# A table of rank offsets for a list-scheduled attention and two-MLP kernel

## The chip, the cores and the metric

The kernel runs on one core of a Trainium2 chip. The time is device microseconds of one launch; the time before is the median of three runs. A profile is one more execution of the same program, recorded by the hardware profiler, and its span is the time from the first to the last instruction.

## What is computed

Attention over 4 batches, 8 heads, 576 positions and 64 channels, in which each row of scores keeps only what lies within `tau` of its maximum, is followed by two multilayer perceptrons with 512 channels and 2048 hidden units, over 2304 tokens. Everything is in float32.

```python
def _attn_ref(q, k, v, tau):
    scores = np.matmul(q, k.transpose(0, 1, 3, 2)) / np.sqrt(q.shape[-1])
    thresh = np.max(scores, axis=-1, keepdims=True) - tau
    scores = np.where(scores >= thresh, scores, -1000000000.0)
    attn = np.exp(scores - np.max(scores, axis=-1, keepdims=True))
    attn = attn / (np.sum(attn, axis=-1, keepdims=True) + 1e-09)
    return np.matmul(attn, v)

def _moe_ref(x, w_in, w_out, s, b):
    r = np.maximum(x @ w_in, 0.0)
    return (s * (r * r) + b) @ w_out

def _moe2_ref(x, w_in, w_out, alpha):
    h = x @ w_in
    return (np.maximum(h, 0.0) + alpha * np.minimum(h, 0.0)) @ w_out
```

## The kernel before, in words

The kernel doesn't issue its work where the code names it. The code describes 7186 steps with `Plan.add` (L131): for each the engine that may run it, an estimate of its duration, the buffers it reads and writes, and a rank. A few kinds may go to one of two engines. `Plan.run` (L154) then goes through a made-up time: whenever an engine is free it takes, of the steps whose inputs are there, the one of the lowest rank, if buffers for it are free, and issues its instructions. Two steps of equal rank go in the order in which they were named. So the result is one fixed order of instructions per engine. On the chip each engine works through its own order, and a step whose input is late holds up all that stands behind it on that engine. The engines are TensorE (PE), VectorE (DVE), ScalarE (ACT), GpSimd (POOL) and SyncE (SP), which issues nearly all DMAs.

The ranks set what counts as urgent. In the attention there are 144 turns, one for each 128 query rows of a pair of heads. Each has a score matmul (L799), a maximum (DVE, L809), an exponential (ACT, L813), a threshold with sum (DVE, L815), transposes through TensorE (L317 and L319), split copies into a high and a low part (ACT and DVE, L952 to L985) and products with the values (L919). The turns are ten ranks apart, so an offset of 10 is one turn. The first four pairs of heads run in plain float32, the others in split float32r. The weights of the first perceptron are read as 64-bit words and converted (`numbers`, L406: a load, L408, then steps at L424 to L437). Their ranks run from 50 on, so that they come in beside the attention.

The perceptrons use three matmuls per product (`mm3`, L540 to L542: low by high, high by low, high by high). Blocks of the first perceptron have rank 1,000,000 and more, and fill TensorE when the attention has nothing for it. From about 500 us on the products of the remaining blocks stand in a chain, each named as coming after the one before (`full[0]`), so the order on TensorE is given there. They are Strassen products in Winograd's form: seven products of half the size, with sums of operands made on DVE and POOL (L505, L1249, L1254), split copies (L517, L518), and sums of results. The latter go so: a product lands in a bank, ACT copies it out (`copy`, L1440, rank `SOON` = -1, into one of at most six tiles of a group called q), and a later product adds onto the same bank, which it may do only after that copy. DVE adds the copy to another bank (`plus`, L1444, rank -1), and `leaky` (L1400) then makes the activation with two steps of ACT and one of DVE (L1405 to L1407, rank -1) and a store (L1409). Nearly everything off TensorE has rank -1 in this part, so the order of naming decides there.

Beside it run the loads of the activations of the next blocks (`load_x`, L546, DMA issue at L551, rank -1), whose halves are added by L1249. There are also the second perceptron's weights, converted to float32 and written back (`whole`, L524, ranks from 200, the multiplication at L424 on ACT or DVE), and the closing steps of the first perceptron's blocks (`outs_of`, L1171: a load of a partial result at L1184, a bias on ACT at L1186, a sum on DVE at L1188, a store at L1191).

A step's number is its place in the order of the calls of `Plan.add`, from 0. The numbers below were found by counting those calls; the order on each engine that results was laid beside the trace. The steps that are spoken of are these: 3920 and 3921, load and multiplication (L424) of one block of weights; 4455 to 4460, loads of activations (L551); 4855 and 4856, load (L1184) and bias step (L1186) of a partial result; 5221, 5340, 5413 and 5979, copies of a product (L1440); 5415 and 5416, the sum (L1444) and first activation step (L1405) of another; 5968, 5969, 5974 and 5975, activation steps; 5451, 5454, 5469 and 5472, split copies (L517); 3939 and 3945, multiplications like 3921 of later blocks of weights.

## Time and profile before

| | us |
|---|---|
| median of 3 runs | 1095.63 |
| lowest and highest | 1094.72, 1096.96 |
| the profiled execution, its own time | 1097.13 |
| its span | 1095.3 |
| TensorE, matmuls busy | 1068.3 (98%) |
| TensorE, weight loads busy | 1011.0 (92%) |
| VectorE busy | 913.7 (83%) |
| ScalarE busy | 785.6 (72%) |
| GpSimd busy | 360.6 (33%) |

The busy times are unions over the span. Matmuls overlap in the pipeline and their ends are modelled, so a matmul that is listed as busy may in part be waiting. The idle time of an engine is what is left of the span. A wait is put down to the instruction whose semaphore came last.

### The profile page before, as it was taken

The page shows a single profiled execution, that of the slowest core. Times are in us where ns is not written, and L with a number is a line of the kernel's source. Part 1 is how long each engine was busy: PE and PEld are TensorE (multiplying, and loading weights), DVE is VectorE, ACT ScalarE, POOL GpSimd, SP SyncE. Part 2 cuts the span into 40 slices and gives each one's busy share as a digit, 9 for nine tenths or more (in the row PEclk, how much of TensorE's full clock was granted, in tenths as well). Part 3 has the DMA queues.
Part 4 walks back from the last instruction along what each step waited for, and adds up shares of the span by engine and source line. Part 5 has one row for each costly group of instructions (what it writes and reads, how often), then busy time and mean ns, then how long its engine had stood idle before and what let it go on. Part 6 is the DMA issues. An engine that isn't in the chain of part 4 may idle for free.

```text
span 1095.3 us, 21723 instructions
## 1 busy us (share of the span) xinstructions
PE 1068.3 (98%) x7070; PEld 1011.0 (92%) x7070; DVE 913.7 (83%) x2075; ACT 785.6 (72%) x1873; POOL 360.6 (33%) x495
## 2 busy tenths in 40 slices
PE   9999999999999999999999999999999999999998
PEld 8777799999989888889999989999999999999998
DVE  4889888888888878848788898799899999998872
ACT  4898888887787778745656676777878997555551
POOL 1455654564575456520000122140102332112111
PEclk9999999999999999999999999999999999999999
DMA  5755375556546454325346976267776564564531
GB/s 119 197 174 161 90 180 136 126 139 187 132 109 162 118 132 99 98 92 183 110 149 225 286 257 201 81 210 251 249 246 224 162 210 137 156 165 126 149 88 39
DMA packets 197489, 174.06 MB, mean 159 GB/s; under 512 B 73472, under 2 KB 175872, under 8 KB 197376
## 3 DMA queue, kind: packets, MB, share of 16 engines
q1 hardware_dynamic: 195072, 171.05, 54.0%
q10 hardware_dynamic: 2304, 1.64, 0.6%
q8 instruction: 55, 0.90, 0.4%
q14 instruction: 58, 0.48, 0.1%
HBM read 100.54 MB, written 50.86 MB: 138 GB/s over the span
## 4 chain that ended last, share of the span: by engine, by line
PE 72%; DVE 10%; DMA 7%; ACT 6%; issue 3%; POOL 0%; SPq 0%; DVEq 0%; ACTq 0%; POOLq 0%
PE bank L540 11%; PE bank L541 11%; PE bank L542 11%; PE bank_b L540 7%; PE bank_b L541 6%; PE bank_b L542 6%; PE bank L919 6%; PE sc L799 6%; PE bank L319 3%; PE bank L317 3%; DMA stg<-in_moe_w_out_dram 2%; DVE e L815 1%; DMA stg<-in_moe_w_in_dram 1%; DVE mx L809 1%; ACT e L813 1%
## 5 line engine op out<-in xcount | busy, mean ns | idle before, releaser
L815 DVE SCALAR_TENSOR_TENSOR e<-sc,mx,e 128x576 f32<-128x576 f32 x144 | 116.1, 812 | 19.2 <-ACT e L813 14.5
L809 DVE TENSOR_REDUCE mx<-sc 128x1 f32<-128x576 f32 x144 | 106.7, 751 | 18.6 <-PE sc L799 17.8
L813 ACT ACTIVATE e<-sc,mx 128x576 f32<-128x576 f32 x144 | 106.1, 743 | 12.9 <-DVE mx L809 12.0
L540 PE MATMUL bank<-gt,wa 128*128 128x384 f32 (+4 forms) x256 | 89.2, 348 | 0.3 <-ACT rest L1065 0.3
L319 PE MATMUL bank<-eyes_r,e 128*128 128x128 f32 (+1 forms) x320 | 89.1, 286 | 0.3 <-DVE e L815 0.3
L540 PE MATMUL bank<-xt,wa 128*128 128x480 f32 (+3 forms) x223 | 84.0, 377 | 5.5 <-ACT gw L1440 4.0
L542 PE MATMUL bank<-gt,wa 128*128 128x384 f32 (+4 forms) x256 | 86.1, 336 | 0.0
L541 PE MATMUL bank<-gt,wa 128*128 128x384 f32 (+4 forms) x256 | 86.0, 336 | 0.0
L541 PE MATMUL bank<-xt,wa 128*128 128x480 f32 (+3 forms) x223 | 75.3, 338 | 0.0
L542 PE MATMUL bank<-xt,wa 128*128 128x480 f32 (+3 forms) x223 | 75.3, 337 | 0.0
L811 POOL TENSOR_SCALAR mx<-mx,tau_s 128x1 f32<-128x1 f32 x144 | 45.6, 317 | 83.1 <-DVE mx L809 77.4
L919 PE MATMUL bank<-gl,vt 128*128 128x256 f32 (+1 forms) x192 | 64.3, 336 | 1.0 <-DVE gl L977 0.7
L919 PE MATMUL bank<-gh,vt 128*128 128x256 f32 (+1 forms) x192 | 57.3, 300 | 1.2 <-ACT gh L975 0.4
L799 PE MATMUL sc<-k,q 128*128 128x288 f32 x264 | 54.7, 335 | 1.2 <-DVE e L815 0.8
L987 POOL TENSOR_TENSOR gr<-gf,gh 64x256 fp32r<-64x256 f32 (+1 forms) x48 | 39.2, 817 | 41.9 <-DVE gl L985 34.4
L540 PEld LDWEIGHTS bank<-xt,wa 128*128 128x128 f32 x223 | 43.1, 193 | 10.1 <-ACT gw L1440 3.0
L977 DVE TENSOR_TENSOR gl<-bank,gh 128x256 fp32r<-128x256 f32 (+1 forms) x96 | 43.4, 452 | 9.8 <-ACT gh L975 8.7
L540 PEld LDWEIGHTS bank<-gt,wa 128*128 128x128 f32 x256 | 49.1, 192 | 1.2 <-ACT rest L1065 0.5
L542 PEld LDWEIGHTS bank<-gt,wa 128*128 128x128 f32 x256 | 48.4, 189 | 1.7
L541 PEld LDWEIGHTS bank<-gt,wa 128*128 128x128 f32 x256 | 48.5, 190 | 0.8
L319 PEld LDWEIGHTS bank<-eyes_r,e 128*128 128x128 f32 (+1 forms) x320 | 44.5, 139 | 4.6 <-DVE e L815 0.7
L975 ACT ACTIVATE gh<-bank 128x256 fp32r<-128x256 f32 (+1 forms) x96 | 39.6, 412 | 11.4 <-PE bank L319 9.9
(729 smaller groups left out, 4203.5 us busy)
## 6 DMA issues: line engine op xcount, KB each, us to landing
stg<-in_moe_w_in_dram SPq DMA_DIRECT2D x32, 512.0 KB, 4.2
stg<-in_moe_w_out_dram SPq DMA_DIRECT2D x32, 512.0 KB, 4.1
gf<-gw SPq DMA_DIRECT2D x41, 192.0 KB, 2.5
q<-hq SPq DMA_DIRECT2D x24, 256.0 KB, 3.9
qo<-hq SPq DMA_DIRECT2D x24, 256.0 KB, 4.7
gw<-gf SPq DMA_DIRECT2D x48, 128.0 KB, 3.0
xt<-xs SPq DMA_DIRECT2D x13, 384.0 KB, 5.4
yat<-ya SPq DMA_DIRECT2D x24, 192.0 KB, 3.8
```

Source lines behind the costliest of these rows:

```text
L319: nc.tensor.transpose(to, part(x), one)
L540: nc.tensor.matmul(o, lhsT=wl, rhs=mh, start=first, stop=False, skip_group_check=on_top)
L541: nc.tensor.matmul(o, lhsT=wh, rhs=ml, start=False, stop=False, skip_group_check=on_top)
L542: nc.tensor.matmul(o, lhsT=wh, rhs=mh, start=False, stop=last, skip_group_check=on_top)
L799: nc.tensor.matmul(sp.t[:, x, :HS], lhsT=o[0][:, c], rhs=o[1][:, x * HS:(x + 1) * HS], start=n == 0, stop=n == len(passes) - 1)
L809: add("DVE", dve(S), lambda sp=sp, mx=mx: nc.vector.tensor_reduce(mx.t[:, 0:1], sp.t[:, :, :HS], op=ALU.max, axis=AX.XY, negate=True), (sp ...
L811: t2 = add("POOL", 0.26, lambda mx=mx: nc.gpsimd.tensor_scalar(mx.t[:, 1:2], mx.t[:, 0:1], -1.0, tau_s, op0=ALU.mult, op1=ALU.subtract), ( ...
L813: add("ACT", act(S, 1), lambda sp=sp, mx=mx, e=e: nc.scalar.activation(halves(e.t), sp.t[:, :, :HS], AF.Exp, bias=mx.t[:, 0:1]), (sp, mx), ...
L815: add("DVE", dve(S) + 0.065, lambda sp=sp, mx=mx, e=e, col=col, sums=sums: nc.vector.scalar_tensor_tensor(halves(e.t), sp.t[:, :, :HS], mx ...
L919: nc.tensor.matmul(o.t[:, :n], lhsT=w.rearrange("p a b -> p (a b)"), rhs=m.t[:, :n], start=c == first and x == 0, stop=c == last and x == ...
L975: add("ACT", act(n), lambda hi=hi, gt=gt: nc.scalar.activation(hi.t[:, :n], gt.t[:, :n], AF.Copy), (gt,), (hi,), rank=rank)
L977: add("DVE", dve(n), lambda hi=hi, lo=lo, gt=gt: nc.vector.tensor_tensor(lo.t[:, :n], gt.t[:, :n], f32(hi.t[:, :n]), op=ALU.subtract), (gt ...
```

## The change

A table `MOVES` is added that gives 2473 of the 7186 steps an offset in rank, 1230 of them positive (later) and 1243 negative (earlier), from 0.0001 to over 100 in size. `Plan.add` adds the offset to the rank of each way in which the step may run. Nothing else is changed: the same steps, instructions, buffers and transfers. Of the table only the lines stand here that hold the steps named in the text, and its first and last line.

```diff
--- before.py
+++ after.py
@@ -45,6 +45,228 @@
 FIRST_CS = (0, 2), (1, 3)
 SECOND_FS = (0, 1, 3, 2, 4, 5)
 LATER = 1e6
+MOVES = {
+    62: 2.91, 63: 2.63, 65: 19.4, 66: 19.4, 67: 15.5, 68: 15.5, 69: 12.3, 70: 12.3, 71: 14.1, 74: 2.32, 76: 0.114, 96: 0.472, 98: 0.822, 99: 1.41,
...
+    3892: -17.7, 3896: -1.88, 3897: 0.276, 3898: -3.45, 3899: -3.08, 3900: -1.48, 3901: -3.45, 3919: -15.3, 3920: 30.8, 3921: 1.38, 3922: -6.27,
...
+    4442: 0.626, 4443: -6.73, 4444: 0.0143, 4447: -6.13, 4448: 0.0143, 4452: 0.0143, 4453: -6.57, 4454: 17.2, 4455: 29.8, 4456: 30.9, 4457: 31.3,
...
+    4458: 13.9, 4459: 37.2, 4460: 28.6, 4461: -26.5, 4462: -51, 4463: 1.45, 4464: -31.4, 4471: -32.9, 4472: 0.382, 4474: -11.1, 4475: 0.382,
...
+    4840: 91.5, 4841: 66.9, 4853: 0.158, 4854: 30.8, 4855: -22.5, 4856: 11.2, 4858: -7.79, 4859: -25.7, 4860: 11.2, 4861: -6.78, 4862: 13.6,
...
+    5360: -29.3, 5371: 1.56, 5397: 0.0404, 5399: 0.0404, 5401: 0.671, 5403: -2.12, 5407: -0.0618, 5408: 11.2, 5409: 2.51, 5412: -6.72, 5413: -26.1,
...
+    5414: -5.78, 5415: -76, 5416: 78, 5417: -14.1, 5418: -16.1, 5419: 0.141, 5420: -19.9, 5422: 48.1, 5423: 1.32, 5424: 20.4, 5425: -60.3, 5426: -65,
...
+    5450: -36.3, 5451: -2.73, 5452: 3.38, 5453: -5.41, 5454: -44.8, 5455: -7.66, 5456: 1.1, 5457: -3.82, 5458: -1.03, 5460: -4.67, 5461: 0.338,
...
+    5977: 1.71, 5978: 1.6, 5979: -0.55, 5980: -14.6, 5982: -0.133, 5985: -1.43, 5986: 1.71, 5991: -1.64, 5997: -0.213, 5998: 1.71, 5999: 1.53,
...
+    7105: -0.135, 7115: -4.19, 7116: -13.9, 7117: -4.19, 7118: -4.53, 7120: -0.343, 7123: -0.343, 7126: 3.06, 7180: 3.44,
+}
 WHOLE, FOR_X = (1, 10), 5
 
 
@@ -136,7 +358,7 @@
         t.fn, t.next, t.tail, t.engine, t.port, t.wire = fn, [], tail, None, port, wire
         n = len(self.tasks)
         ways = [(engine, us, n if rank is None else rank)] if isinstance(engine, str) else engine
-        t.ways = [(e, u, (r, n)) for e, u, r in ways]
+        t.ways = [(e, u, (r + MOVES.get(n, 0), n)) for e, u, r in ways]
         t.bufs = list(dict.fromkeys([*reads, *writes]))
         deps = set(after)
         for b in reads:
```

## Rows read from the trace of the kernel before

**Rows 1.** Page, part 1: busy us (share of the span), instructions, of each engine.

```profile
PE 1068.3 (98%) x7070; PEld 1011.0 (92%) x7070; DVE 913.7 (83%) x2075; ACT 785.6 (72%) x1873; POOL 360.6 (33%) x495
```

**Rows 2.** Stretches: bounds and length, busy us (instructions) by engine, TensorE clock, DMA, GB/s.

```profile
0.00:15.00 15.00, 13.28 (x58) 12.13 (x59) 3.37 (x13) 3.69 (x6) 3.13 (x18) 1.00 0.54 118
15.00:150.00 135.00, 128.85 (x802) 104.12 (x802) 118.59 (x260) 114.55 (x263) 74.56 (x97) 1.00 0.57 153
150.00:500.00 350.00, 344.04 (x2433) 317.51 (x2432) 283.25 (x659) 266.52 (x620) 181.74 (x271) 1.00 0.52 133
...
900.00:1000.00 100.00, 99.56 (x807) 99.25 (x807) 96.36 (x269) 64.12 (x183) 21.61 (x21) 1.00 0.55 153
1000.00:1095.30 95.30, 90.85 (x758) 90.65 (x756) 60.37 (x170) 39.70 (x107) 12.35 (x16) 0.99 0.34 92
```

**Rows 3.** Waits of TensorE, 500 to 1000 us: total us, times, longest.

```profile
PE bank L540 <- ACT gw L1440: 4.0, 3, 2.0
PE bank_b L540 <- DVE yb L1188: 1.7, 3, 0.8
PE bank_b L540 <- DVE gw L1309: 1.4, 2, 0.7
PE bank L540 <- ACT of L1440: 0.9, 1, 0.9
PE bank_b L540 <- ACT yat L1440: 0.4, 1, 0.4
```

**Rows 4.** Waits of TensorE, 15 to 500 us: the two largest.

```profile
PE sc L799 <- DVE e L815: 2.9, 5, 0.9
PE bank L919 <- ACT z L999: 2.1, 3, 1.0
```

**Rows 5.** Timeline of ScalarE, 776 to 790 us: start, duration, idle before it.

```profile
781.39 0.67 ACT L426 ACTIVATE n<-stg 128x512 f32<-128x512 f32 x1 [0.65 <-DMA stg<-in_moe_w_out_dram]
...
784.12 0.49 ACT L1440 ACTIVATE gw<-bank 128x384 f32<-128x384 f32 x1
```

**Rows 6.** Timeline of TensorE, 779 to 789.5 us.

```profile
779.35 0.33 PE L542 MATMUL bank<-xt,wa 128*128 128x384 f32 x1
...
784.76 0.41 PE L540 MATMUL bank<-xt,wa 128*128 128x384 f32 x1 [1.95 <-ACT gw L1440]
```

**Rows 7.** Stretches right after that wait, as in rows 2.

```profile
785.70:789.10 3.40, 3.40 (x12) 3.40 (x12) 3.00 (x6) 3.19 (x9) 0.00 (x0) 0.50 0.70 164
789.10:795.00 5.90, 5.90 (x35) 5.90 (x35) 4.44 (x7) 4.98 (x13) 3.00 (x3) 1.00 0.53 181
```

**Rows 8.** Timeline of ScalarE, 725.5 to 733 us.

```profile
729.39 0.61 ACT L1186 ACTIVATE yat<-yat,bias 128x384 f32<-128x384 f32 x1 [1.15 <-DMA yat<-ya]
729.91 0.47 ACT L1440 ACTIVATE gw<-bank 128x384 f32<-128x384 f32 x1
```

**Rows 9.** Timeline of TensorE, 729 to 733 us.

```profile
730.43 0.44 PE L540 MATMUL bank<-xt,wa 128*128 128x384 f32 x1 [1.34 <-ACT gw L1440]
```

**Rows 10.** Timeline of ScalarE, 758.5 to 763 us.

```profile
760.00 0.66 ACT L426 ACTIVATE n<-stg 128x512 f32<-128x512 f32 x1 [1.80 <-DMA stg<-in_moe_w_out_dram]
```

**Rows 11.** Timeline of ScalarE, 903 to 906.8 us.

```profile
905.64 0.47 ACT L1440 ACTIVATE yat<-bank_b 128x384 f32<-128x384 f32 x1
```

**Rows 12.** Loads of L551, 600 to 640 us: issues, who waited (us, times), us to landing.

```profile
L551 SPq DMA_DIRECT2D xt<-xs x6: 378/452/567, 613.1 to 639.7; - x6
...
  POOL gw L1249: 9.2, 1
...
DMA to landing us min/median/max: 3.2/5.5/6.4
```

**Rows 13.** Groups of TensorE by line and shape, count | busy us, mean ns | idle before.

```profile
L319 PE MATMUL bank<-eyes_r,e 128*128 128x128 f32 x304 | 84.9, 287 | 0.3 <-DVE e L815 0.3
...
L542 PE MATMUL bank<-gt,wa 128*128 128x384 f32 x103 | 35.1, 341 | 0.0
...
L799 PE MATMUL sc<-gw 128*128 128x288 f32 x36 | 10.2, 406 | 0.0
```

210 rows, old and new, of the table MOVES are left out of this document.

## The prediction, made before the changed kernel was run

> **What bounds the kernel now.** I read the page's first part, then the table by stretches, then TensorE's waits, and last the timelines around the longest of them. TensorE is listed busy for 1068.3 of 1095.3 us [rows 1], so 27.0 us of the span are its visible idle time. The reader should see where they lie [rows 2]. The first 15 us hold 1.7, in which the first loads come in. The stretch 15 to 150 holds 6.2 (135.00 - 128.85), 150 to 500 holds 6.0, and the last stretch 4.5, which is the copying out of the last results. No order of issue takes away the work before the first transposes or behind the last matmul, so some 20.9 us can be reached by a reordering. The other engines are no free reserve: VectorE is busy for 118.6 of 135 us in the attention's first stretch and for 96.4 of 100 after 900 us [rows 2].
>
> The waits say what ends this idle time. After 500 us it is above all ScalarE's copies of products, 4.0 us in three waits, and the sums that close a block on VectorE, 1.7 and 1.4 us [rows 3]. Before 500 us it is a score bank that VectorE has not yet released, 2.9 us in five waits, and an output bank of the values' product, 2.1 us in three [rows 4]. No wait is over 2 us, and there are dozens: the change has no large target, only many small ones.
>
> **What the change can do at the waits that the trace shows.** A rank counts only where two steps can be had at the same time, so I looked at each of the long waits for the step that released TensorE, at what its engine did between that step's input and its start, and at the table's entries for both.
>
> The longest wait. A product ends about 779.7 us (its last matmul starts at 779.35 and takes 0.33), and its copy runs only at 784.12, 4.4 us later. TensorE stands still for 1.95 us for it [rows 5, 6]. In between ScalarE ran eight steps, among them two weight multiplications (3939 and 3945), before the first of which it waited 0.65 us for a load [rows 5]. The table gives the copy, step 5413, -26.1. Of the eight only the split copy 5454 (-44.8) keeps a lower rank, and the activation step 5416, which also wants a tile of the copy's pool, gets +78. There is a second price: right behind this wait twelve matmuls took 3.40 us at half of TensorE's clock (0.50), where 35 took 5.90 us after it (0.17 each) [rows 7], so 3.40 - 12 x 0.17 = 1.4 us went there. But the copy had the lower rank of most of these steps before the change too (-1 against -0.997 and 304). It stood back because no tile of its group was free, and an offset frees none; it only puts the copy first in line for the next one. Bounds 0 and 3.35 us; I take the middle, 1.7, since both the tile and the order are at work.
>
> The second, at 730.4 us: 1.34 us [rows 9]. The copy 5221 could run at 727.0, but stood behind the bias step 4856 with the same rank -1, for which ScalarE waited 1.15 us until a load landed, and which then took 0.61 [rows 8]. The table gives 4856 +11.2, so the copy passes it, and its load 4855 -22.5, so that this comes sooner. Bounds 0 and 1.76 us (1.15 + 0.61); I take 1.3, the wait itself.
>
> The third, 0.9 us at 762 us [rows 3]. ScalarE waits 1.80 us for a block of weights [rows 10], then works off four activation steps ahead of the copy 5340. The load, 3920, gets +30.8 and so comes behind later blocks, but its multiplication hardly moves (+1.38). If the multiplication stays where it is, it waits longer. Bounds -0.9 and +0.9; half of the upper one, 0.45, because the multiplication may also go to VectorE, or stand later once its load does.
>
> The fourth, 0.4 us at 906 us [rows 3]. The copy 5979 (-0.55) ran at 905.64 [rows 11]; it passes the four activation steps right ahead of it: 5968 (+0.49), 5974 and 5975 (0) and 5969 (-0.25). 0.4 us, with nothing in its way.
>
> The sums that close a block, 1.7 + 1.4 = 3.1 us [rows 3]. The steps on VectorE that release these banks have entries of both signs. A quarter, 0.8, between 0 and 3.1.
>
> The attention, 12.1 us (6.15 + 5.96) [rows 2]. Most of the waits there are chains that begin at once when their input is there: an exponential, then the threshold, then the bank is free [rows 4]. Passing does nothing for such a chain. It helps only if TensorE has other work in front of it, which the table can do with the blocks of the first perceptron. Bounds 0 and 12.1; I take a quarter, 3.0, nearer to the low end because VectorE is at 88% there.
>
> New waits. 2473 offsets shift hundreds of small meetings that fit today. The unit of such a miss is one wait of the size of those in [rows 4], 0.6 to 1.0 us; I book -1.0 and leave up to -8 to the rival below. The table issues no more instructions, and a DMA that moves on SyncE's queue costs the same issue at another time. The start and the last 4.5 us stay.
>
> Sum: 1.7 + 1.3 + 0.45 + 0.4 + 0.8 + 3.0 - 1.0 = 6.65 us. The profiled execution's own time was 1097.13 us, 1.8 over its span and 1.5 over the median of the runs. 1097.13 - 6.65 = 1090.5 with the profiler, and 1.5 less, 1089.0 us, as the median. What comes next once these waits go is TensorE itself: from 500 us on its order is a chain, and it would be busy all through.
>
> **A rule that counts the reserve differently.** Busy matmuls hide waiting here: transposes of 128 columns are listed at 287 ns each, matmuls of 384 columns at 341 [rows 13]. Weight loads are busy for only 1011.0 us [rows 1], and between 15 and 500 us for 421.6 of 485, against 472.9 of matmuls [rows 2]. The Trainium skill ("Trainium Kernel Development and Optimization", Performance Expectations) holds matmul busy time for a bad measure, since matmuls are pipelined, and wants weight-load busy time read in its place. By that rule a quarter of the attention's idle time would be 15.8 us and not 3.0, and the sum 19.4 us. Against it, from this trace: the first four pairs work in plain float32, whose score matmuls are listed at 406 ns for 288 columns [rows 13], and such long matmuls leave the loader idle without any wait. So I keep the first count for the forecast, and the second as a rival.
>
> **Rivals.**
> Slower, by late loads. The loads of activations 4455 to 4460 get +13.9 to +37.2, at a rank that was -1 like that of everything around them. From 613.1 us on they are issued into the second buffers, land 5.5 us after issue in the median, and GpSimd waited 9.2 us for one of them [rows 12]: nothing is in hand there. Behind every load and store of rank -1, each by one flight later, the two dependent rounds come 2 x 5.5 = 11 us later, TensorE has only the closing products of the last pair to fill that with, and the 6.65 us of the forecast turn into a loss of 11.0 - 6.65 = 4.35: 1100.0 us. It decides from a slip of 6.65 us on, which is one flight and a fifth. Against it: SyncE's queue is seldom long, and a rank counts only while something else is ready.
> No change. The chains on TensorE and a VectorE at 88 and 96% [rows 2] give each wait back within the same stage, or the planner, which counts a rank only among steps that are ready, restores most of the old order, so that the table doesn't do what it says. The time is then 1095.6, within 2.2 us.
> A deeper gain. The table packs the transposes and products of the attention also where matmuls are listed as busy while they wait [rows 13]. A quarter of 485 - 421.6 = 63.4 us is 15.8 in place of 3.0: 1089.0 - 12.8 = 1076.2 us.
>
> **How the numbers follow.** The forecast, 1089.0, has a chance of 0.62; its own bounds are 1078, if half of the 20.9 us and all of the 1.4 of the clock come back along with some of what the matmuls hide, and 1093, if only the surest two (1.3 and 0.4) stand with little else. The deeper gain has 0.08, no change 0.12, slower 0.18. About 0.2%, 2.2 us, can be told from no change in a measurement of this kernel. So faster is 0.62 + 0.08 = 0.70, the same 0.12, slower 0.18. The range of 8 in 10 goes from 1078 to 1099: below it lies most of the deeper gain, above it somewhat over half of the slower case.
>
> **What would show it.** In the profile of the changed kernel: copies of L1440 no longer among the first waits after 500 us, and their sum 4.0 down to 1 to 2 us; no stretch of half clock between 700 and 800 us; the bias step of L1186 behind the copy around 730 us; idle time between 15 and 500 us down from 12.1 to about 9. Of the total idle time, 27.0 us, about 20 to 22 should be left. Wrong would be: idle time after 600 us that ends with a DMA of L551 or with L1249 (the slower rival); idle time as before in other places (no change); or weight-load busy time between 15 and 500 us in clearly fewer us of span (the deeper gain). Also, if the profile's whole loss or gain lies in the first 150 us, my count of the single waits was beside the point, since I put only part of 3.0 us there.

## The result and the profile after

The changed kernel takes 1082.3 us (median of 4 runs, 1078.9 to 1083.2) against 1095.4 for the kernel before: a ratio of 0.9873 [0.9849, 0.9897], 13.1 us less. The forecast was 1089.0, 6.4 less. The profiled execution is the fastest of the four, 1078.93 us with a span of 1077.1, while that of the kernel before, 1097.13, lies above all its other runs. So the two profiles are 18.2 us apart where the medians are 13.1 apart, and some 5 us of what the profiles show is spread between executions. One execution of e1_early below, 1141.0 us at a mean granted clock of 0.85, is a slow one and left out of its figures.

The lines of the new file are 222 higher: L540 is now L762, L799 is L1021, L1440 is L1662, L1309 is L1531, L551 is L773. The first part of the page of the changed kernel, as in [rows 1]:

```profile
PE 1059.9 (98%) x7070; PEld 1008.8 (94%) x7070; DVE 920.6 (85%) x2093; ACT 781.4 (73%) x1864; POOL 361.3 (34%) x486
```

The span is 18.2 us shorter. TensorE's visible idle time fell from 27.0 us [rows 1] to 17.2, that is by 9.8. The other 8.4 us lie in the matmuls' listed time: 1068.3 before, 1059.9 now, for the same 7070 matmuls. Weight loads took 1011.0 and take 1008.8, so their idle time fell from 84.3 to 68.3, by 16.0: this line shows nearly the whole difference, the matmuls' line about half of it.

Where it comes from: the changed kernel by stretches (bounds and length; busy us and instructions of TensorE's matmuls, its weight loads, VectorE, ScalarE and GpSimd; clock, DMA share, GB/s), to be held against [rows 2]:

```profile
15.00:150.00 135.00, 130.18 (x820) 106.39 (x820) 118.23 (x252) 115.83 (x268) 86.31 (x106) 1.00 0.57 154
150.00:500.00 350.00, 346.62 (x2466) 324.49 (x2465) 292.08 (x686) 271.32 (x623) 173.67 (x261) 1.00 0.53 137
...
600.00:700.00 100.00, 98.71 (x560) 97.03 (x559) 90.93 (x185) 72.34 (x168) 20.11 (x21) 1.00 0.67 222
700.00:790.00 90.00, 89.17 (x511) 88.17 (x510) 85.88 (x171) 71.79 (x168) 14.63 (x13) 1.00 0.72 239
```

and the kernel before in the stretches that [rows 2] leaves out:

```profile
600.00:700.00 100.00, 96.89 (x548) 94.90 (x547) 84.73 (x167) 69.08 (x154) 18.04 (x17) 1.00 0.68 221
700.00:790.00 90.00, 85.14 (x477) 83.89 (x476) 81.61 (x162) 69.91 (x166) 16.22 (x19) 0.98 0.68 216
```

From 15 to 500 us the matmuls' idle time went from 12.1 us (6.15 + 5.96) to 4.82 + 3.38 = 8.2, only 3.9 less. But in the same 485 us 51 more matmuls ran, and the loader was busy for 430.9 us in place of 421.6: 9.3 us more work. Between 600 and 790 us the kernel before idled for 3.1 + 4.9 us, the changed one for 1.3 + 0.8.

TensorE's waits in the changed kernel from 500 us to the end (total us, times, longest), against [rows 3]:

```profile
PE bank_b L762 <- ACT gw L1662: 0.8, 1, 0.8
PE bank L762 <- DVE gw L1531: 0.7, 1, 0.7
PE bank_b L762 <- DVE gw L1531: 0.7, 1, 0.7
```

and from 15 to 500 us, the two largest, against [rows 4]:

```profile
PE sc L1021 <- issue: 1.6, 1, 1.6
PE bank L1117 <- DVE gl L1207: 0.8, 1, 0.8
```

ScalarE's copies (L1440, now L1662) cost TensorE 5.3 us in [rows 3] (4.0 + 0.9 + 0.4) and 0.8 now. The score banks that VectorE held (2.9 us, [rows 4]) have left the top of the list.

For a finer count each step was found in each trace by the order of issue, and the planner's estimates of TensorE's steps that had started by a time were added up. By how many us of work a kernel is ahead of the one before (profiled runs):

| by (us) | 100 | 200 | 300 | 400 | 500 | 600 | 650 | 700 | 800 | 850 | 1050 |
|---|---|---|---|---|---|---|---|---|---|---|---|
| changed kernel | 2.4 | 4.3 | 6.4 | 7.8 | 10.5 | 10.4 | 12.5 | 12.0 | 17.7 | 18.7 | 18.0 |

So there are two gains: 10.5 us grow steadily in the attention, and some 8 more come between 600 and 850 us. Behind that nothing changes.

Two more readings belong to this table. First, the runs e1, e6, e9, e10 and e11 below have exactly the changed kernel's order of the steps below 3650 (the work of about the first 490 us) on every engine, and yet their leads by 500 us are 8.9, 8.4, 9.4, 5.8 and 6.3 us. So the attention's gain is some 6 to 10 us, and the profile above shows its upper end. The matmuls' idle time from 15 to 500 us varies as much with one and the same order: 8.2 us above, 11.0 in e10:

```profile
15.00:500.00 485.00, 473.96 (x3269) 427.51 (x3269) 407.54 (x928) 384.93 (x884) 259.50 (x367) 1.00 0.54 139
```

Second, from step 5220 on, the first product of the second perceptron, TensorE's 420 remaining steps stand in the same order before and after. Step 5220 starts at 725.8 us before and at 713.8 in the changed kernel, 12.0 us sooner; step 5559, the 73rd of the 420, starts at 808.3 and at 790.4, 17.9 us sooner. So 5.9 us of the second gain come in a stretch in which TensorE does the same work in the same order. That stretch before, and in the changed kernel:

```profile
725.80:808.30 82.50, 77.64 (x434) 76.39 (x434) 76.61 (x146) 64.57 (x151) 13.36 (x15) 0.98 0.73 231
```

```profile
713.80:790.40 76.60, 75.77 (x433) 74.77 (x433) 72.48 (x140) 63.96 (x148) 11.45 (x11) 1.00 0.77 254
```

TensorE's idle time fell there by 4.0 us, from 4.9 to 0.8, and the 1.4 us that the half clock had cost [rows 7] are gone: 4.0 + 1.4 = 5.4 of the 5.9.

### The profile page after: what moved, and what is told of

It is laid out like the page before. It is cut to its first block, busy times and chain, and to the rows that moved or that the text cites. A ratio compares the mean times of both kernels' runs of the same rounds, so it can differ in the third digit from the quotient of the medians.

```text
span 1077.1 us, 21727 instructions
## 1 busy us (share of the span) xinstructions
PE 1059.9 (98%) x7070; PEld 1008.8 (94%) x7070; DVE 920.6 (85%) x2093; ACT 781.4 (73%) x1864; POOL 361.3 (34%) x486
## 4 chain that ended last, share of the span: by engine, by line
PE 84%; DVE 6%; ACT 4%; DMA 3%; issue 2%; SPq 0%; POOL 0%; DVEq 0%; POOLq 0%; ACTq 0%
PE bank L762 13%; PE bank L764 12%; PE bank L763 12%; PE bank_b L762 8%; PE bank_b L763 8%; PE bank_b L764 8%; PE sc L1021 7%; PE bank L1141 7%; PE bank L541 4%; PE bank L539 3%; DMA stg<-in_moe_w_in_dram 1%; DVE e L1037 1%; PE bank L1117 1%; DMA stg<-in_moe_w_out_dram 1%; DVE n L656 1%
## 5 line engine op out<-in xcount | busy, mean ns | idle before, releaser
L762 PE MATMUL bank<-gt,wa 128*128 128x384 f32 (+4 forms) x230 | 80.7, 351 | 0.3 <-ACT rest L793 0.3
L762 PE MATMUL bank<-xt,wa 128*128 128x480 f32 (+3 forms) x212 | 79.0, 373 | 0.3 <-ACT rest L793 0.3
L1033 POOL TENSOR_SCALAR mx<-mx,tau_s 128x1 f32<-128x1 f32 x144 | 49.9, 348 | 83.7 <-DVE mx L1031 74.1
L764 PE MATMUL bank<-gt,wa 128*128 128x384 f32 (+4 forms) x230 | 76.8, 334 | 0.0
L763 PE MATMUL bank<-gt,wa 128*128 128x384 f32 (+4 forms) x230 | 76.8, 334 | 0.0
L764 PE MATMUL bank<-xt,wa 128*128 128x480 f32 (+3 forms) x212 | 71.4, 337 | 0.0
L763 PE MATMUL bank<-xt,wa 128*128 128x480 f32 (+3 forms) x212 | 71.3, 336 | 0.0
L1021 PE MATMUL sc<-k,q 128*128 128x288 f32 x280 | 58.1, 333 | 2.3 <-issue 1.6
L1021 PEld LDWEIGHTS sc<-k,q 128*128 128x128 f32 x280 | 43.4, 190 | 7.0 <-issue 1.8
L656 DVE SCALAR_TENSOR_TENSOR n<-stg,n 128x512 int32<-128x512 int32 x64 | 46.9, 736 | 0.8
L1194 POOL TENSOR_TENSOR gl<-gf,gh 128x256 fp32r<-128x256 f32 (+1 forms) x48 | 39.3, 820 | 21.9 <-DVE gh L1193 15.3
L764 PEld LDWEIGHTS bank<-gt,wa 128*128 128x128 f32 x230 | 43.3, 188 | 1.7
```

The source lines that it names most:

```text
L656: add("DVE", dve(DM), lambda: nc.vector.scalar_tensor_tensor(ni(), word(0), 29, ni(), op0=ALU.logical_shift_right, op1=ALU.bitwise_or), (n ...
L762: nc.tensor.matmul(o, lhsT=wl, rhs=mh, start=first, stop=False, skip_group_check=on_top)
L763: nc.tensor.matmul(o, lhsT=wh, rhs=ml, start=False, stop=False, skip_group_check=on_top)
L764: nc.tensor.matmul(o, lhsT=wh, rhs=mh, start=False, stop=last, skip_group_check=on_top)
L1021: nc.tensor.matmul(sp.t[:, x, :HS], lhsT=o[0][:, c], rhs=o[1][:, x * HS:(x + 1) * HS], start=n == 0, stop=n == len(passes) - 1)
L1033: t2 = add("POOL", 0.26, lambda mx=mx: nc.gpsimd.tensor_scalar(mx.t[:, 1:2], mx.t[:, 0:1], -1.0, tau_s, op0=ALU.mult, op1=ALU.subtract), ( ...
```

## The experiments

All edits are to the changed kernel's table, if nothing else is said, and leave everything else as it is. The planner is part of the kernel: its own made-up clock ends at 1070.2 for the kernel before and 1055.4 for the changed one, and the table at the end of this section sets its end beside the chip's time for each.

**Halves of the table.** Step 3650 is the first that belongs to the work from about 500 us on.

```diff
+MOVES = {n: r for n, r in MOVES.items() if n < 3650}     # e1_early, 1190 entries
+MOVES = {n: r for n, r in MOVES.items() if n >= 3650}    # e2_late, 1283 entries
```

> Only the table's entries of steps below 3650 (attention, first perceptron's weights, first four blocks: the first 500 us) are kept. Theory A (most of the gain is in the attention's part, where matmuls that are listed as busy hide waiting): about 10.5 us faster than before, some 1085. Theory B (the named waits behind 500 us carry the gain, as the forecast's sum had it): 2 to 3 us faster, some 1093.

> Only the entries of steps from 3650 on (everything from about 490 us on) are kept. Theory A: what is left, 13.1 less some 10, so 3 to 7 us faster, 1088 to 1092, with the waits for L1440 copies and the half clock at 786 us gone. Theory B: about 10 us faster, some 1085. If e1 and e2 together give much more or less than the whole table, the parts are not independent.

Measured: e1_early 1089.7 us, ratio 0.993 [0.9905, 0.9955]; e2_late 1098.5, ratio 1.0023 [1.0008, 1.0038]. The whole gained 13.1, the first half 5.9 (against the median of before in the same set, 1095.5) to 7.7 (by the ratio), and the second half alone loses 2.5. The halves don't add up: the second is worth 5 to 7 us behind the first and less than nothing without it. The first half loses part of its lead at one place. Its stretches:

```profile
15.00:500.00 485.00, 476.69 (x3285) 430.59 (x3284) 409.55 (x934) 385.96 (x887) 259.96 (x367) 1.00 0.54 141
600.00:700.00 100.00, 95.15 (x535) 92.52 (x534) 83.17 (x165) 68.43 (x154) 17.50 (x17) 1.00 0.65 208
```

In the attention it does as much as the whole table (loader 430.59, there 430.88). By 600 us it is 9.4 us ahead, by 650 only 6.2. Where the whole table idles for 1.3 us between 600 and 700, it idles for 4.85.

**The named entries.** Those twelve on which my single waits rested.

```diff
+MOVES = {n: MOVES[n] for n in (3920, 3921, 4855, 4856, 5413, 5415, 5416, 5451, 5454, 5968, 5969, 5979)}
```

> Only twelve entries: those of the steps that the forecast's four named waits turn on. The forecast's sum (1.7 + 1.3 + 0.45 + 0.4) wants 3.9 us faster, 1091.5. The rival, that these waits end on free tiles and that a single offset only moves the wait, wants no difference (within 2 us of 1095.4).

Measured: 1097.3 us, ratio 1.0021 [1.0006, 1.0037]. The waits of TensorE from 500 us on in this kernel (L763 is L540 of before, L1663 is L1440):

```profile
PE bank L763 <- ACT gw L1663: 2.2, 4, 0.8
PE bank_b L763 <- DVE yb L1411: 2.0, 4, 0.6
PE bank_b L763 <- ACT gw L1663: 1.6, 2, 0.9
PE bank_b L763 <- DVE gw L1532: 1.4, 2, 0.7
PE bank L763 <- ACT of L1663: 0.8, 1, 0.8
PE bank L763 <- ACT yat L1663: 0.8, 1, 0.8
```

Three of the four waits went as I had said: the copy 5413 starts 0.9 us after its product (before 4.4, whole table 0.6), 5221 after 1.0 us (before 2.9, whole table 1.2), 5979 after 0.9 us (before 2.0, whole table 0.6). The third did not: the copy 5340 starts 2.3 us after its product (before 2.4, whole table 0.8), and TensorE waits 0.8 us for it. No wait is over 0.9 us, and the clock stays at 1.00 from 700 to 790 us. But waits for such copies sum to 2.2 + 1.6 + 0.8 + 0.8 = 5.4 us, where [rows 3] has 4.0 + 0.9 + 0.4 = 5.3: they are shorter, more, and mostly for copies of other products. Step 5559 starts 82.1 us after step 5220 (before 82.5, changed kernel 76.6), and nothing was gained.

**The loads, alone and left out.**

```diff
+MOVES = {n: MOVES[n] for n in range(4455, 4461)}                      # e4_loads
+MOVES = {n: r for n, r in MOVES.items() if not 4455 <= n <= 4460}    # e6_no_loads
```

> Only the entries of the six loads of activations 4455 to 4460 (+13.9 to +37.2). The slower rival of the forecast wants 5.5 to 11 us more, 1101 to 1106. The other side, that a rank counts only among steps that are ready and SyncE's queue is rarely long, wants no difference (1093 to 1097).

> The whole table without the six load entries 4455 to 4460, which alone made the kernel 6.8 us slower (e4). Rival E (each entry has its own worth, which adds up): 6 us or so faster than the whole table, some 1076. Theory C (fitted to one another; the plan's end goes to 1065.8 from 1055.4): about 10 us slower than the whole table, some 1092.

Measured: e4_loads 1103.4 us, ratio 1.0062 [1.0041, 1.0083]; e6_no_loads 1095.1, ratio 0.9991 [0.9976, 1.0006]. Alone the six entries cost 7 to 8 us, as the slower rival said. In the whole table they are worth some 12: without them it gains nothing. Between 600 and 660 us e4_loads, then the kernel before:

```profile
600.00:660.00 60.00, 53.54 (x287) 52.10 (x287) 50.48 (x98) 36.86 (x78) 10.77 (x11) 0.94 0.80 263
```

```profile
600.00:660.00 60.00, 57.70 (x324) 56.03 (x323) 52.97 (x102) 43.32 (x95) 10.93 (x10) 1.00 0.83 271
```

Alone, idle time grows there from 2.3 to 6.5 us, and the clock's mean falls to 0.94. e6_no_loads has the whole lead of the attention (8.9 us by 600) and keeps 3.1 of it by 650.

**The attention without TensorE's own entries.** Of the first half only the entries of steps on the other engines, 801.

```diff
+MOVES = {n: r for n, r in MOVES.items() if n < 3650}
-        t.ways = [(e, u, (r + MOVES.get(n, 0), n)) for e, u, r in ways]
+        t.ways = [(e, u, (r + (MOVES.get(n, 0) if e != "PE" else 0), n)) for e, u, r in ways]
```

> The entries below step 3650 without those of TensorE's steps: 801 of 1190. Theory C (the entries are fitted to one another, and the plan's own made-up time sees it: its end is at 1070.2 us before the change, 1055.4 with the whole table, 1058.8 with the first part, and 1070.0 with this one): no gain, 1093 to 1098. Rival D (the gain of the first 500 us comes from the order on ScalarE and VectorE, whose copies TensorE waits for): most of e1's 7.6 us stays, about 1089.

Measured: 1094.2 us, ratio 0.9983 [0.9967, 0.9999]. Its stretch from 15 to 500 us:

```profile
15.00:500.00 485.00, 475.79 (x3242) 424.22 (x3242) 400.14 (x916) 384.87 (x884) 266.71 (x375) 1.00 0.54 141
```

The matmuls' idle time is down to 9.2 us, close to the whole table's 8.2 (and below the 11.0 of e10, which has the whole attention part), but the loader did only 2.6 us more than before, where the runs with the whole attention part did 5.9 (e10) to 9.3. To go by the visible idle time this would be three quarters of the attention's gain; by the loader, and by the time, it is about a quarter. So most of the attention's gain needs the entries of TensorE's own steps, and it doesn't show in the idle time between matmuls but in what is listed as busy.

**Is this hidden time free for anything?** To the kernel before 160 matmuls with 61,440 columns in all were added, whose results are overwritten by the next product: in e7_more_att in the first blocks, beside the attention, in e8_more_late from 495 us on, behind it.

```diff
-    def hidden(xs, n, fs, units, rank, last=()):
+    def hidden(xs, n, fs, units, rank, last=(), again=0):
...
+                    for _ in range(again if c == 0 else 0):
+                        nc.tensor.matmul(h.t[:, i * n:(i + 1) * n], lhsT=u.w_in(1, c, f), rhs=x.t[:, 0, :n], start=True, stop=True)
...
-                h, last = hidden(x, n, (f,), u1i, LATER + j, full)
+                h, last = hidden(x, n, (f,), u1i, LATER + j, full, 4)     # e7_more_att
...
-                h, full[0] = hidden([x_of[j][c] for c in range(NC)], n, (f,), u1i, seq[0], (last if i == 0 and f < 4 else full[0],))
+                h, full[0] = hidden([x_of[j][c] for c in range(NC)], n, (f,), u1i, seq[0], (last if i == 0 and f < 4 else full[0],), 8)     # e8_more_late
```

> The kernel before, in its own order, with 160 matmuls more in the first perceptron's first four blocks (the first matmul of each hidden unit is made four times more and overwritten): 40 x (120 + 148 + 217 + 217) ns = 28.1 us of TensorE at the spacing of the trace, all of it between 90 and 460 us. If TensorE is as busy there as it is listed (12.1 us idle in 15 to 500), it costs at least some 20 us, 1116 or more. If matmuls that are listed as busy hide waits, clearly less, 8 to 18 us.

> The control for e7: the same number of matmuls more, 160 of 384 columns, 160 x 173 ns = 27.7 us, in the two blocks that run behind the attention (495 to 575 us), where weight loads are busy too for 99 of 100 us. Both theories: nearly the whole price, 25 to 28 us, 1121 to 1124.

Measured: +22.8 us beside the attention (ratio 1.0208 [1.0176, 1.024]) and +26.8 behind it (1.0245 [1.0217, 1.0272]). So the attention swallows at most some 4 us more of them (the two intervals overlap), though the loader is idle there for 63.4 us [rows 2] and for 0.9 us in the 100 us behind 500. The groups of the added matmuls, e7_more_att (count | busy us, mean ns | idle before):

```profile
L565 PE MATMUL bank<-xt,wa 128*128 128x480 f32 x80 | 21.7, 393 | 0.2
L565 PE MATMUL bank<-xt,wa 128*128 128x320 f32 x40 | 8.1, 323 | 0.3 <-ACT rest L573 0.2
L565 PE MATMUL bank<-xt,wa 128*128 128x256 f32 x40 | 7.9, 319 | 0.1
```

They stand in one piece with the other products of their block. With e5_early_no_pe this fits an idle time that lies between the attention's own steps, so that only an order that puts other steps right there uses it; these runs don't show it by themselves. Another reading stands beside it: 30.9 of the 63.4 us lie before 150 us [rows 2], where the four plain float32 pairs run, and part of that may be no waiting at all. In the changed kernel the loader's gain is 2.3 us before 150 us and 7.0 behind.

**Which of the loads.** e9_no_4457 takes one entry of the whole table away, e10_two_loads replaces the six by two small ones that only swap the loads of each pair.

```diff
+MOVES.pop(4457)                                                                    # e9_no_4457
+MOVES = {n: r for n, r in MOVES.items() if not 4455 <= n <= 4460}                  # e10_two_loads, with the next line
+MOVES.update({4458: -0.5, 4460: -0.5})
```

> The whole table without one of its 2,524 entries, that of load 4457 (+31.3). Without it 4457 is again issued ahead of 4458, so that the next set of loads, 4459 and 4460, has to wait for the copy that follows 4458 rather than for that of the earlier load; the kernel's own planner ends its made-up clock at 1065.8 in place of the whole table's 1055.4. Theory A (the order of the six loads decides whether the gain of the attention part is kept through 600 to 650 us; the loads themselves cost nothing by their lateness): load 4459 and 4460 land near 618 to 621 us as in the run without all six entries, the weights' sums of the first Strassen product come 4 to 6 us later than in the changed kernel, and the time is 1092 to 1097. Theory B (one entry among 2,524 is noise; the run without the six entries was slow because 4455 and 4456 then came too early for the buffers): 1082 to 1085, as the changed kernel.

> The whole table with its six entries for loads 4455 to 4460 (+20.8, +44.3, +31.3, +13.9, +56.7, +39.2) taken out and two put in their place: 4458 and 4460 by -0.5 rank, which only puts each ahead of its neighbour of the pair. No load is named late any more. Theory A (only the order within the two pairs matters): 1080 to 1085, as the changed kernel, with 4459 and 4460 landing near 611. Theory B (the loads have to be late, so that the queue is free for the weight loads beside them): 1090 to 1097, as the run without the six entries.

(The table has 2473 entries, not 2,524, and the six are +29.8, +30.9, +31.3, +13.9, +37.2 and +28.6; the figures in these two texts were wrong. Nothing hangs on them.)

Measured: e9_no_4457 1093.2 us, ratio 0.9985 [0.9967, 1.0002]; e10_two_loads 1080.9, ratio 0.986 [0.9823, 0.9898]. One entry of 2473 decides some 11 us, and that the loads are late does not matter, only their order. (In e10's profile, which is 3.6 us less ahead at 600 us than the changed kernel's, 4460 and 4459 land at 615.0 and 616.0 us and not near 611.) What that order does is seen on SyncE's queue (start, us, line, operation). In the changed kernel:

```profile
603.11 1.80 SPq L773 DMA_DIRECT2D xt<-xs  x3
609.68 0.33 SPq L1413 DMA_DIRECT2D yf<-yb  x1
```

in e9_no_4457 (one line further down in the file):

```profile
603.47 0.65 SPq L774 DMA_DIRECT2D xt<-xs  x1
610.04 0.33 SPq L1414 DMA_DIRECT2D yf<-yb  x1
...
613.21 1.19 SPq L774 DMA_DIRECT2D xt<-xs  x2
```

load_x names the next set of loads as coming after the last-named of the set before (L546 to L554: `chain[0] = (t,)`), and the planner waits for that. With 4458 issued ahead of 4457 that condition is met sooner, so that 4460 and 4459 go out at 603.8 and 604.5 us, ahead of a store for which the queue then stands until 609.7. With 4457 first 4459 and 4460 come behind that store, at 613.2 and 613.8, and land at 619.9 and 621.2 in place of 611.6 and 610.6. The Strassen product of step 4505 starts at 627.9 in place of 621.4. What TensorE then waits for between 600 and 700 us in e9_no_4457, and the stretches around it:

```profile
PE bank L763 <- DVE yb L1411: 3.5, 2, 2.9
PE bank_b L763 <- ACT wa L1480: 2.4, 1, 2.4
```

```profile
620.00:630.00 10.00, 6.54 (x27) 5.53 (x26) 10.00 (x18) 5.10 (x11) 2.99 (x3) 0.83 0.95 346
630.00:640.00 10.00, 6.54 (x31) 5.89 (x30) 8.44 (x17) 5.08 (x11) 1.33 (x1) 0.89 0.84 243
640.00:650.00 10.00, 10.00 (x56) 10.00 (x55) 7.94 (x14) 5.53 (x13) 2.18 (x3) 0.94 0.67 229
```

It stands for 6.9 us from 620 to 640, for banks that closing sums release and for a split copy of the weights' sums. Right behind the waits of 2.44 and 1.03 us, and again behind that of 2.91, the granted clock is at the lower of its two levels (0.50, that is 1.2 in place of 2.4 GHz) for 3.4 us each, which makes the means of 0.83, 0.89 and 0.94 above:

```profile
624.08:627.50 3.42, 3.23 (x9) 2.79 (x10) 3.42 (x9) 3.20 (x8) 0.65 (x1) 0.50 1.04 393
637.74:641.15 3.41, 3.41 (x11) 3.41 (x12) 2.38 (x6) 1.43 (x3) 0.00 (x0) 0.50 1.02 285
```

Of a lead of 9.4 us by 600, 2.1 are left by 650.

**Are the two loads what the attention lacks, and do they help alone?**

```diff
+MOVES = {n: r for n, r in MOVES.items() if n < 3650} | {4458: -0.5, 4460: -0.5}   # e11_early_two
+MOVES = {4458: -0.5, 4460: -0.5}                                                  # e12_two_alone
```

> Only the entries of steps below 3650 (the attention part, 1,190 entries) and the two loads 4458 and 4460 by -0.5 rank. The planner's made-up clock ends at 1060.0 (attention part alone: 1058.8; whole table: 1055.4). Theory A (the two loads are what the attention part lacks to keep its gain through 600 to 650 us, the 1,300 other entries do little): 1081 to 1085. Theory B (the swapped loads help only together with the entries around them, which make the weights' multiplications and copies of that stage fit; so the late part is worth some 6 us of its own): 1087 to 1092, as the attention part alone at 1089.9.

> The kernel before with two entries only, loads 4458 and 4460 by -0.5 rank. The planner's clock ends at 1071.4 (before: 1070.2). Theory A (the swap sends the next pair of loads ahead of a store for which SyncE's queue stands, and so gains by itself): 1088 to 1092. Theory B (it is worth something only where the work before it comes 9 to 10 us sooner, since in the kernel before these loads find their buffers and their data just in time): 1094 to 1098, no change.

Measured: e11_early_two 1089.2 us, ratio 0.9934 [0.9909, 0.9959], like the attention part without them; e12_two_alone 1096.7, ratio 1.0008 [0.9994, 1.0022], no change, though 4459 and 4460 go out at 614.7 and 615.7 us there in place of 620.7 and 621.2. So the swap is needed by something else in the late entries. The longest wait of e11_early_two from 500 us on:

```profile
PE bank_b L763 <- DVE yb L1411: 3.2, 1, 3.2
```

L1411 is L1188 of before: TensorE stands for a bank until a closing sum of the block before has released it.

**Which entries carry the gain.** Entries were dropped from the table one after another as long as the planner's clock did not end later. 137 were left, 109 below step 3650 and 28 above. Of the 28, 19 belong to TensorE: 17 are products of the second half of a perceptron block that add onto a bank (`into`, L1193 of before, matmuls at L540 to L542), 2 are Strassen products. e15 drops these 19, e14 keeps the 28 alone.

```diff
-MOVES = { ... 2473 entries ... }
+MOVES = {62: 2.91, 74: 2.32, 172: 2.23, ...   # e13_137; the late ones, alone in e14_late_28:
+    4233: 2.27, 4380: 5.33, 4389: 1.51, 4404: -34.3, 4409: 0.878, 4418: 1.8, 4420: 4.02, 4421: 4.02, 4422: 4.02, 4457: 31.3,
+    4459: 37.2, 4471: -32.9, 4476: -121, 4481: -30, 4493: 45.4, 4500: 39.3, 4575: 1.9, 4589: 1.89, 4620: 2.79, 4629: 2.47,
+    4787: 18.2, 4789: 7.63, 4830: 16.6, 4831: 50.1, 4832: 18.2, 4833: 27.8, 4834: 30.3, 4855: -22.5}
```

> 137 of the table's 2,473 entries: 109 below step 3650 and 28 above. They were found by dropping entries as long as the planner's made-up clock did not end later (1055.4, as with the whole table). Theory A (a few entries carry the gain, the rest are without effect on the time): 1079 to 1085, as the whole table. Theory B (the gain is a sum of many small shifts, which the planner's clock doesn't see): 1086 to 1092.

> The 28 late ones of these 137 entries alone, on the kernel before. Planner's clock 1066.7 (before: 1070.2). Theory A (the late part helps by itself once the useless late entries are gone): 1090 to 1093.5. Theory B (it fits only behind the attention part, as the late half of the whole table did, 1098.5): 1094 to 1099.

> The 137 entries without the 19 that belong to TensorE's products behind step 3650. Loads 4457 and 4459 keep theirs, so the pairs of loads stay swapped. Planner's clock 1059.4. Theory A (TensorE's own order after 500 us is not fixed by the chain, and the gain between 600 and 850 us comes from its change): 1085 to 1090, 5 to 8 us more than e13. Theory B (the order of loads and of the sums is what counts there): 1079 to 1084, as e13.

Measured: e13_137 1081.5 us, ratio 0.9893 [0.9874, 0.9911]; e14_late_28 1092.0, ratio 0.9975 [0.9961, 0.999]; e15_137_no_late_pe 1088.6, ratio 0.9949 [0.9933, 0.9965]. A twentieth of the table does what the whole does. Without TensorE's late entries 6 to 7 us of it are lost (1088.6 - 1081.5 = 7.1; 6.1 by the ratios). The stretches 600 to 700 and 700 to 790 us of e13_137, then of e15_137_no_late_pe:

```profile
600.00:700.00 100.00, 98.28 (x561) 97.32 (x560) 85.07 (x178) 72.10 (x168) 21.55 (x22) 1.00 0.67 220
700.00:790.00 90.00, 88.22 (x499) 86.05 (x498) 83.79 (x162) 68.94 (x164) 19.57 (x20) 1.00 0.69 226
```

```profile
600.00:700.00 100.00, 97.22 (x546) 96.10 (x545) 81.45 (x162) 69.19 (x158) 19.69 (x21) 0.98 0.63 213
700.00:790.00 90.00, 85.61 (x481) 82.85 (x480) 83.26 (x161) 70.39 (x169) 21.05 (x23) 1.00 0.66 216
```

In 190 us e13_137 gets through 1060 matmuls, the other through 1027. By the count of steps e13_137 is 9.9 us ahead by 600 and 16.7 by 850, e15_137_no_late_pe 8.3 and 9.4. What the late entries move is seen from the starts of single products in the traces: step 4380 starts at 594.4 us with the attention part alone and at 614.0 with the whole table; 4787 at 677.7 and 699.2; 4620 at 661.0 and 669.4. These products are not in the chain of Strassen products: of TensorE's steps each comes only after the one before it on its bank, so they can be kept back and put between products of the chain. But that holds for the first perceptron alone. In e13 and e15, as in the kernel before and the changed one, step 5220 comes behind all of them, and from there on TensorE's order is the same. Where the 7 us arise is seen from when fixed steps start (us):

| kernel | step 5220 starts | from there to step 5559 |
|---|---|---|
| before | 725.8 | 82.5 |
| changed | 713.8 | 76.6 |
| e1_early | 718.6 | 83.0 |
| e3_named | 725.4 | 82.1 |
| e13_137 | 713.7 | 78.7 |
| e14_late_28 | 721.6 | 78.5 |
| e15_137_no_late_pe | 717.7 | 81.8 |

So 4.0 us are there when the second perceptron begins (1.0 of them by 500 us, up to where the two have the same order), and 3.1 more come in a stretch in which TensorE's order is the same and for whose steps from 4856 on neither table has an entry. What differs there is the planner's order on the other engines, which follows from the earlier shifts. Which of its changes removes the waits was not tested.

**A table pressed further.** Entries were changed at random, and a change was kept by the end of the planner's clock.

```diff
-MOVES = { ... 2473 entries ... }
+MOVES = { ... 6120 entries ... }
```

> A table changed further at random, each change kept or not by the end of the planner's clock, from the whole table's: its end is 1054.2, 1.25 lower than the whole table's. So far the chip's median lay 24 to 31 us above the planner's end. Theory A (the planner's clock foretells the chip, with a scatter of some 3 us): 1078 to 1085. Theory B (a table that fits the planner's clock still better fits the chip worse): above 1085.

Measured: 1084.7 us, ratio 0.9917 [0.99, 0.9934]. A planner's end 1.25 us lower brought nothing; it is in the expected range, but not ahead of the changed kernel. None of the kernels run is clearly ahead of it: e10_two_loads, 1080.9, and e13_137, 1081.5, have the same time within their intervals.

The planner's own end and the chip's median:

| kernel | planner | chip | difference |
|---|---|---|---|
| before | 1070.2 | 1095.4 | 25.2 |
| changed | 1055.4 | 1082.3 | 26.9 |
| e1_early | 1058.8 | 1089.7 | 30.9 |
| e2_late | 1073.5 | 1098.5 | 25.0 |
| e3_named | 1068.6 | 1097.3 | 28.7 |
| e4_loads | 1075.9 | 1103.4 | 27.5 |
| e5_early_no_pe | 1070.0 | 1094.2 | 24.2 |
| e6_no_loads | 1065.8 | 1095.1 | 29.3 |
| e9_no_4457 | 1065.8 | 1093.2 | 27.4 |
| e10_two_loads | 1055.4 | 1080.9 | 25.5 |
| e11_early_two | 1060.0 | 1089.2 | 29.2 |
| e12_two_alone | 1071.4 | 1096.7 | 25.3 |
| e13_137 | 1055.4 | 1081.5 | 26.1 |
| e14_late_28 | 1066.7 | 1092.0 | 25.3 |
| e15_137_no_late_pe | 1059.4 | 1088.6 | 29.2 |
| e16_search | 1054.2 | 1084.7 | 30.5 |

## Why the prediction was right and wrong

The direction and the kind were right, faster and by many waits, and the time lies within the range. The gain, 13.1 us, is twice the 6.65 of the sum. Point by point:

The attention is the term that was mis-sized: 3.0 was booked, and e1_early puts what stays of it in the time at 5.9 to 7.7 us; e15_137_no_late_pe, with 109 of its entries and nine late ones, wins 5.6 to 6.2. The step behind the 3.0 was to take a quarter of the matmuls' visible idle time, 12.1 us, for the reserve. That idle time fell by 3.9 us in the changed kernel and by 1.1 in e10 with the same order, while the loader did 9.3 and 5.9 us more work. e5_early_no_pe shows the two apart: nearly the same visible idle time as the changed kernel, a quarter of the gain. Most of the gain needs the entries of TensorE's own steps, and it lies in matmuls listed as busy, as the rival of the deeper gain had said. That rival was wrong in the size: of the loader's 63.4 us of idle time 5.9 to 9.3 were got, 9 to 15%, where it had put a quarter, a share of my own choosing, and e7_more_att shows that work which is put somewhere in this stretch pays nearly its full price.

The Trainium skill ("Trainium Kernel Development and Optimization", Performance Expectations) calls matmul busy time a bad metric, because matmuls are pipelined, and the busy share of weight loads a good one. As to where the gain shows, this trace agrees: over the whole span the loader's idle time fell by 16.0 us of 18.2, the matmuls' by 9.8.

The single waits (1.7 + 1.3 + 0.45 + 0.4 = 3.85 us) are gone in the changed kernel, as is the stretch at half clock, and their price was not what failed: from step 5220 to 5559, where TensorE's order is the same, 4.0 us less waiting and the 1.4 us of the clock give nearly all of the 5.9 us won. What failed is the step from the entries to the waits. e3_named has the twelve entries that I had read, is rid of three of the four waits, and gains nothing, since TensorE then waits for other copies (5.3 us before, 5.4 there); e13_137 has one of the twelve, 4855, and no entry of a later step, and wins 3.8 us in that stretch. The waits are places at which the chain shows that it waits, not four causes. That the late terms of the sum (3.85 + 0.8 = 4.65 us) come near the 5 to 7 us won behind the attention is therefore luck.

The sentence on what comes next failed in part: that from 500 us on TensorE's order is a chain, as the description of the kernel says too (and, in the slower rival, that TensorE has little to fill a gap with). It is so from step 5220 on, at 714 to 726 us. Before that the Strassen products are a chain, but the products of `into` beside them are not, and the table moves many of them. By e13 and e15 those entries are worth 6 to 7 us in this table, 4.0 of them by step 5220. I had looked at the table's entries for ScalarE, SyncE and VectorE behind 500 us, and for TensorE's at none. Of the closing sums, booked at 0.8, 1.4 of the 3.1 us in [rows 3] are left, so 1.7 went; which entries did that isn't shown.

New waits were booked at -1.0. The changed kernel has one of 1.6 us and a few of 0.6 to 0.8 in the attention that were not there before; what they cost was not measured apart, since the attention's gain is counted with them.

The signs that I had set came out: copies down from 4.0 to 0.8 us, no half clock between 700 and 800 us, 8.2 us idle between 15 and 500 us, and 17.2 in all, less than the 20 to 22 expected. They could not tell my account from this one.

The slower rival was right for its entries alone: a loss of 7 to 8 us (e4_loads) where it had 4.35 left after the other gains. Its price was that of a late load. In the whole table the same entries are worth some 12 us of gain, and not for being late (e10_two_loads), but for the order within a pair, which takes the next pair past a store for which the queue stands (e9_no_4457). A rival made of one group of entries told nothing of the sign in a table that was fitted as a whole. The rival of no change failed too: VectorE, at 88 and 96% in [rows 2], did not give the waits back.

How far the parts hang together: the 109 attention entries with nine late ones of other engines (e15) win 6.2 us, the 28 late entries alone (e14), which hold the same nine, 2.7, and all 137 (e13) 13.2 in the same set of runs. Some 4.3 us, 3.5 by the ratios, come only with both.

What stays open is which single `into` product fills which wait, what takes the waits behind step 5220 away when TensorE's order there is unchanged, and why e1_early and e16_search lie some 4 us further above the planner's end than the changed kernel does (single executions of e1_early lie between 1084.0 and 1090.4 us, of e16_search between 1082.1 and 1087.5).

## What to carry to other kernels

A table of ranks that was fitted as a whole can't be priced by its entries: 137 of 2473 carried it, one entry less cost 11 us, and the entries that I could explain were worth nothing alone. Where a planner is at hand whose made-up time follows the chip's, it says more than a sum over waits: it put this change at 14.8 us, 13.1 were measured, and over all kernels the chip lay 24 to 31 us above it. The price of a wait can be right while the reason given for its going is wrong; to tell time that is won from waits that move on, compare when one fixed step behind the stretch starts in both traces, and look at a second run of the same order before reading a few us out of one pair of profiles. Look for the steps of the bounding engine that are free to move, and for where they are moved. Read the reserve of a matmul-bound stretch from the weight loads' idle time rather than the matmuls', but as an upper bound.

## What the runs showed of the hardware

The same 61,440 columns of matmul cost 26.8 us behind the attention and 22.8 beside it, though the loader has 63.4 idle us in the latter (e7, e8; the two intervals overlap). Right behind waits of 2.44 and 1.03 us and of 2.91 us the granted clock was 0.50 for 3.4 us (e9), as behind the wait of 1.95 us in [rows 7]; it stayed at 1.00 from 700 to 790 us where no wait was over 0.9 us (e3, and the changed kernel). Two loads that stood behind a store in SyncE's queue went out 9 to 10 us later than ahead of it (4459 at 613.2 against 604.5 us, 4460 at 613.8 against 603.8), though neither needed that store.
